# A filter's magnitude table shared between GpSimd and ScalarE, with a new order of the kernel's head

## The chip, the cores and the metric

The kernel runs on one core of a Trainium2 chip. A core has TensorE (matrix products, with its weight loads counted apart), VectorE, ScalarE and GpSimd for elementwise work, and SyncE, which here only issues DMAs; the profile calls them PE and PEld, DVE, ACT, POOL and SP. Each engine works through its own list of instructions in order and waits on semaphores for the others. The metric is device time in microseconds; the median of several runs is compared. Each kernel is also run once under the hardware profiler, and all rows shown come from such an execution.

## The reference

Two branches of a layer are added to the input. Both start from the same layer norm, over 2048 tokens of width 448.

```python
def _A_ref(u, log_A_real, A_imag, C_real, C_imag, log_dt, D_skip):
    dt = jnp.exp(log_dt)
    A = -jnp.exp(log_A_real) + 1j * A_imag          # [448, 256]
    C = (C_real + 1j * C_imag) * dt[:, None]
    P = jnp.exp((A * dt[:, None])[:, :, None] * pos[None, None, :])   # pos = 0 .. 2047
    K = 2.0 * jnp.einsum("dn,dnl->dl", C, P).real   # a filter of 2048 taps for each channel
    y = irfft(rfft(u_t, 2 * L) * rfft(K, 2 * L))[:, :, :L]
    return y + u * D_skip

def _B_ref(x, w_gate, w_up, w_down):                # width 448 -> 1792 -> 448
    h = _sigmoid(x @ w_gate) * (x @ w_up)
    return h @ w_down

xn = _layernorm(A_u)
return A_u + _A_ref(xn, ...) + _B_ref(xn, ...)
```

Everything is float32.

## The kernel before

Two Python generators, `conv()` (branch A) and `glu()` (branch B), are traced in turn, by weights that say how far each has come; a planner then works out the order of the instructions on every engine from the dependencies, the order of tracing, the priorities (`hp(HP)` raises them) and its own costs. `tc.issue_after(ins)` adds one rule by hand: what the block traces on the engine of `ins` is queued behind `ins`. So the order of each queue is fixed before the run, and it is worked out anew when an instruction changes.

**Head** (`conv`, from line 987). The tokens are handled in four groups of four blocks (a block is 128 tokens). `x_load` (232) brings a group into `accs[0]`, then `accs[1]`, one DMA for each 32 partitions; the first group's four go over SP and ScalarE's queue. On SP follow the gate and up weights of the first two slices of the hidden width (`w_load`), the down weights (`rd_load`), the parameters of the filter and groups 2 and 3. For groups 0 and 1 VectorE then takes mean and variance of each block (`x_stats`, 236), makes the scales with small steps that end in `zs` (`x_scales`, 253), and VectorE and ScalarE scale the blocks in turn (`x_norm`, 260 and 262). `x_transpose` (191) turns the group on TensorE; ScalarE copies the result to a rounded tile `xh` (or `xr`, 215, for the last 64 rows) and VectorE keeps the rest in `xl` (213, 216). A product is three matmuls with such pairs, high by high, high by low and low by high.

**Branch B** (`glu`, 691). For each of 14 slices f of the hidden width, `gate` (657) multiplies by the gate and up weights (670), ScalarE takes a tanh (678), VectorE forms `hf` and ScalarE and VectorE split it into `hh` and `hl` (686, 688). The down weights are split by ScalarE's `dh` (745) and GpSimd's `dl` (746) and multiplied later (777). In the first group of slices the order is f = 0, f = 1 for the first half of the tokens and then f = 0, f = 1 for the second, so that the second transposes are needed a little later. `marks[0]` is the latest tanh.

**Filter** (`prep`, then `kgen`, 434). `prep` turns the parameters into phases, gains `GG` and decays `W1` on VectorE, ScalarE and GpSimd. `kgen` then walks over 56 chunks of 8 channels. For each channel and state there is a decay r (one table of it in `me`, with the entries r^0 to r^63, and one in `mf`, with the gain times powers of r^64); `powers` (423) makes r^1, r^2, r^4 ... in `pm` for 8 chunks at a time, the row `pm[:, 6]` being filled with ones. `magnitudes` (469) makes the tables for two chunks on GpSimd: each step multiplies the finished half of the table by one power and so doubles it, with 1, 2, 4, 8, 16, 32 entries for each of 32 columns in `me` (w in the code). There are two buffers of `me` and `mf`. `ahead` (499) makes angles on TensorE (507) and sine and cosine in `S` on ScalarE (516 to 519). VectorE multiplies tables and S into `Et` (566, 567) and `Ft` (568), and TensorE contracts these over the states (578) into `ko`; every four chunks a first stage of the transform follows (534, 540). Chunks alternate with branch B's matmuls on TensorE's queue.

**Transform** (`spectra`, 799), from about 606 us: products of the spectra and the way back, together with the second half of branch B.

Of the kernel before, what the change touches and what calls it, by code (L numbers as in the profile page):

```python
# [47 lines left out]
DC = 8  # L48
# [82 lines left out]
def s4d_glu_kernel(ctx, tc, io):  # L131
# [59 lines left out]
    def x_transpose(src, xs, o0):  # L191
# [4 lines left out]
        for k in range(4):  # L196
# [10 lines left out]
            if k == 1 and nb == 2:  # L207
                p = ps.rearrange("p (k t) -> p k t", k=2)
                nc.scalar.copy(xh[:, 0:2, o], p)
                v.tensor_tensor(xl[:, 0:2, o], p, xh[:, 0:2, o], ALU.subtract)  # L210
            elif k < 3:
                nc.scalar.copy(xh[:, k, o], p)
                v.tensor_tensor(xl[:, k, o], p, xh[:, k, o], ALU.subtract)  # L213
            else:
                nc.scalar.copy(xr[0:64, o], p)
                xls[:] = [v.tensor_tensor(xr[64:128, o], p, xr[0:64, o], ALU.subtract)]

# [216 lines left out]
    def kgen(pk):  # L434
# [34 lines left out]
        def magnitudes(b):  # L469
# [16 lines left out]
            for m, base, nst in ((me, 0, 6), (mf, 7, 5)):  # L486
                for i in range(1 if m is mf else 0, nst):
                    w = 1 << i
                    with tc.issue_after(mls[0].ins) if mls else nullcontext():
                        ins = nc.gpsimd.tensor_tensor(  # L490
                            m[:, :, w : 2 * w],
                            m[:, :, 0:w],
                            par(base + i).unsqueeze(2).to_broadcast([128, 4 * DC, w]),
                            ALU.mult,
                        )
            mls[:] = [ins]
# [51 lines left out]
        nc.gpsimd.memset(mes[1][:, :, 0:1], 1.0)  # L548
        yield 4
        for g in range(NCK // NCH):  # L550
            for c in range(NCH):
# [3 lines left out]
                if c == 4 and NCH * (g + 1) < NCK:  # L555
                    if g == 0:
                        pms.append(pqs[0].tile([128, 12, NCH * 2 * DC], F32, name="pm1", tag="u0"))
                        nc.gpsimd.memset(pms[1][:, 6], 1.0)
                    with tc.issue_after(fts[0].ins):
                        powers(pms, g + 1)  # L560
# [12 lines left out]
                for q in range(2):  # L573
                    sl = 2 * (cn % 4) + q
                    for k in range(4):
                        h, cc = k // 2, k % 2
                        for j in range(4):
                            nc.tensor.matmul(  # L578
# [112 lines left out]
    def glu():  # L691
        for half in range(2):
# [4 lines left out]
            for fs_ in ORDER[half]:  # L697
# [14 lines left out]
                for n_, (f, t) in enumerate(order):  # L712
# [26 lines left out]
                    if t == 0:  # L739
                        dh = pg.tile([128, D], F32R, name="dh", bufs=FCH[0])  # L740
                        if half == 0:
                            rd = rd or rd_load(f)
                            dl = d_low()
                            with hp(HP), tc.issue_after(marks[0].ins):
# [232 lines left out]
    def conv():  # L977
        with tc.tile_pool(name="psk", bufs=1, space=PSUM) as ps_, tc.tile_pool(
# [9 lines left out]
            with tc.tile_pool(name="pst", bufs=1, side="right", reuse_waits="tile") as pst:  # L988
# [7 lines left out]
                x_load(accs[0], 0, 4, [nc.sync, nc.scalar])  # L996
# [10 lines left out]
                for q in range(2):  # L1007
                    xn = slots[f"xn{q}"]
                    with hp(HP):
                        for b in range(4 * q, 4 * q + 4):  # L1010
                            x_stats(sm, b, accs[q][:, b % 4])
# [55 lines left out]
    W1s, GGs = [], []  # L1067
# [43 lines left out]
```

## Time and profile before

| | |
|---|---|
| median of 3 runs | 799.61 us (797.79 to 801.61) |
| profiled execution | 803.19 us, span of its instructions 801.4 us |
| busy in the span | TensorE 716.8, VectorE 583.9, ScalarE 399.0, GpSimd 400.8 us |
| mean granted TensorE clock | 0.956 |
| head and preparation, 0 to 128 us | TensorE idle for about half of the first 40 us, then in one gap between 60 and 80 |
| chunk loop, 128 to 606 us | 28 table calls on GpSimd, 56 chunks |
| transform, 606 to 801 us | TensorE busy nearly throughout |

The busy time of an engine is the sum of its instructions; matmuls are pipelined, so a busy TensorE is not one at its peak. Rows by time give the start and length in us, the engine, the line of the kernel, the tiles (written <- read), the shape and in brackets the idle time before it with what ended it. In the chain of waits each moment is given to the instruction that the end of the work last waited for.

### The profile page before, as it was taken

Reading aid. Unit: us, or ns where it says so; the run is one execution under the profiler, and the core shown is the slowest. Engines: PE = TensorE matmul, PEld = TensorE weight load, DVE = VectorE, ACT = ScalarE, POOL = GpSimd, SP = SyncE. Lnnn points to the kernel's source line nnn. Section 1 sums busy time; section 2 is a strip of 40 time slices with the busy share of each in tenths; the row PEclk is TensorE's granted clock in tenths of the full one; section 3 lists DMA queues with packets and bytes.
Section 4 is the critical chain, followed back from the end, with each engine's and each line's share of the span. In section 5 each row is a group of like instructions: output and inputs, shape, how many; then the busy total and the mean of one; then the engine's idle time right before and its main releaser. Section 6 shows DMA issues by size and latency. Waiting matters only on the chain.

```text
span 801.4 us, 19239 instructions
## 1 busy us (share of the span) xinstructions
PE 716.8 (89%) x7892; PEld 563.5 (70%) x7892; DVE 583.9 (73%) x776; ACT 399.0 (50%) x594; POOL 400.8 (50%) x423
## 2 busy tenths in 40 slices
PE   1896998859798898969999899998999999998995
PEld 1674787648687787746587687787787777776783
DVE  4598996788897989888655977996794555545453
ACT  2645464654665765777626646754742332231320
POOL 1120055998855885884374568669364400243001
PEclk9997999959899999999899999999999999999998
DMA  9926347103522444434485132222145998999736
GB/s 208 226 76 180 103 133 225 38 15 127 165 85 67 150 147 119 118 93 147 119 239 174 62 97 90 64 85 91 59 133 167 285 246 218 227 233 258 179 110 167
DMA packets 90568, 114.74 MB, mean 143 GB/s; under 512 B 11825, under 2 KB 78577, under 8 KB 90225
## 3 DMA queue, kind: packets, MB, share of 16 engines
q1 hardware_dynamic: 81264, 92.78, 42.1%
q10 hardware_dynamic: 6640, 14.57, 6.0%
q0 software_dynamic: 2576, 6.17, 2.9%
q8 instruction: 62, 1.02, 0.5%
q14 instruction: 26, 0.20, 0.1%
HBM read 69.64 MB, written 43.84 MB: 142 GB/s over the span
## 4 chain that ended last, share of the span: by engine, by line
PE 52%; DVE 16%; POOL 9%; DMA 4%; issue 4%; ACT 4%; SPq 1%; ACTq 0%; POOLq 0%; DVEq 0%
PE gu L670 19%; PE po L777 13%; PE sp L859 6%; POOL me L490 5%; PE ko L578 5%; PE tr L507 4%; PE pv L886 3%; DVE Et L567 3%; DVE Ft L568 3%; POOL mf L490 2%; DVE pm L429 2%; DVE hl L688 1%; DVE Et L566 1%; PE gu L271 1%; DMA acc_d<-acc 1%
## 5 line engine op out<-in xcount | busy, mean ns | idle before, releaser
L490 POOL TENSOR_TENSOR me<-me,pm 128x32 f32<-128x32 f32 (+1 forms) x168 | 176.4, 1050 | 134.7 <-DVE Et L567 122.0
L490 POOL TENSOR_TENSOR mf<-mf,pm 128x64 f32<-128x64 f32 (+1 forms) x112 | 116.0, 1036 | 4.0
L566 DVE TENSOR_TENSOR Et<-me,S 128x1024 f32<-128x1024 f32 x56 | 84.9, 1516 | 44.2 <-ACT S L519 35.3
L670 PE MATMUL gu<-xh,wh 128*128 128x512 f32 x336 | 103.3, 414 | 3.9 <-DVE xl L213 3.2
L670 PE MATMUL gu<-xh,wl 128*128 128x512 f32 x336 | 99.2, 402 | 0.0
L670 PE MATMUL gu<-xl,wh 128*128 128x512 f32 x336 | 96.5, 393 | 0.0
L777 PE MATMUL po<-dh,hh 128*128 128x448 f32 x224 | 87.2, 389 | 1.8 <-DVE acc L782 1.8
L578 PEld LDWEIGHTS ko<-Et,Ft 128*32 128x32 f32 x3584 | 56.6, 115 | 43.8 <-issue 29.5
L516 ACT ACTIVATE S<-tr 128x1024 f32<-128x1024 f32 x56 | 57.3, 1024 | 59.5 <-PE tr L507 54.4
L578 PE MATMUL ko<-Et,Ft 128*32 128x64 f32 x3584 | 66.6, 228 | 22.3 <-DVE Ft L568 20.9
L568 DVE TENSOR_TENSOR Ft<-mf,S 128x1024 f32<-128x1024 f32 x56 | 83.8, 1496 | 2.0 <-POOL mf L490 2.0
L777 PE MATMUL po<-dl,hh 128*128 128x448 f32 x224 | 85.0, 379 | 0.0
L777 PE MATMUL po<-dh,hl 128*128 128x448 f32 x224 | 84.4, 378 | 0.0
L567 DVE TENSOR_TENSOR Et<-me,S 128x1024 f32<-128x1024 f32 x56 | 83.6, 1493 | 0.0
L688 DVE TENSOR_TENSOR hl<-hf,hh 128x512 fp32r<-128x512 f32 x56 | 58.9, 1052 | 26.6 <-ACT hh L686 26.6
L670 PEld LDWEIGHTS gu<-xh,wh 128*128 128x128 f32 x336 | 61.6, 192 | 23.5 <-issue 5.8
L507 PE MATMUL tr<-sel,ph 128*128 128x512 f32 x224 | 66.3, 419 | 11.3 <-ACT S L518 11.2
L670 PEld LDWEIGHTS gu<-xh,wl 128*128 128x128 f32 x336 | 65.2, 194 | 14.4
L686 ACT CAST hh<-hf 128x512 fp32r<-128x512 f32 x56 | 34.8, 622 | 80.2 <-DVE hf L681 71.1
L670 PEld LDWEIGHTS gu<-xl,wh 128*128 128x128 f32 x336 | 63.8, 190 | 13.7
L782 DVE SCALAR_TENSOR_TENSOR acc<-po,acc 128x448 f32<-128x448 f32 x80 | 48.1, 617 | 30.0 <-PE po L777 30.0
L678 ACT ACTIVATE th<-gu 128x512 f32<-128x512 f32 x56 | 33.5, 599 | 66.0 <-PE gu L670 58.8
(185 smaller groups left out, 1302.0 us busy)
## 6 DMA issues: line engine op xcount, KB each, us to landing
sk_d<-sk ACTq DMA_DIRECT2D x14, 512.0 KB
sx<-x_d SPq DMA_DIRECT2D x32, 224.0 KB
skl<-sk_d SPq DMA_DIRECT2D x16, 448.0 KB
vp<-v_d SPq DMA_DIRECT2D x16, 448.0 KB
v_d<-vt SPq DMA_DIRECT2D x62, 112.0 KB
wt_d<-wh SPq DMA_DIRECT2D x9, 512.0 KB
wt_d<-wl SPq DMA_DIRECT2D x9, 512.0 KB
wh<-wt_d SPq DMA_DIRECT2D x9, 512.0 KB
```

The source lines that it names most:

```text
L490: ins = nc.gpsimd.tensor_tensor(m[:, :, w : 2 * w], m[:, :, 0:w], par(base + i).unsqueeze(2).to_broadcast([128, 4 * DC, w]), ALU.mult,)
L507: nc.tensor.matmul(ps[:, h], ph[:, cn % 2, 128 * h : 128 * h + 128], sel[:, i], start=(i == 0), stop=(i == 1),)
L516: nc.scalar.activation(rows(cs), pv, AF.Abs)
L566: v.tensor_tensor(Et[:, :, :, 32:64], two(me[:, :, 32:64]), S[:, 1::-1], ALU.mult)
L567: v.tensor_tensor(Et[:, :, :, 0:32], two(me[:, :, 0:32]), S[:, 1:3, :, ::-1], ALU.mult)
L568: fts[:] = [v.tensor_tensor(Ft, two(mf), S[:, 3:5], ALU.mult)]
L578: nc.tensor.matmul(ko[32 * j : 32 * j + 32, sl], Ft[:, cc, DC * h + 4 * q + j], Et[:, cc, DC * h + 4 * q + j], start=(k == 0), stop=(k == ...
L670: glu_mm[:] = [nc.tensor.matmul(ps, a_, b_, start=(n == 0), stop=(n == len(mm) - 1))]
L688: v.tensor_tensor(hl, hf, hh, ALU.subtract)
L777: glu_mm[:] = [nc.tensor.matmul(po, a_[:, bs], w_, start=(n == 0), stop=(n == 3 * fc - 1))]
L782: v.scalar_tensor_tensor(acc[:, b], po, 0.5, acc[:, b], ALU.mult, ALU.add)
L859: mm = nc.tensor.matmul(to, tb[:kk, t, 64 * c : 64 * c + 64], rhs, start=True, stop=True, skip_group_check=True,)
```

## The change

Five edits.

- The first group's load becomes two loads of two blocks each, eight DMAs instead of four.
- The statistics of the second group are queued on VectorE behind the first group's norm (`normed` is the last of its scalings on VectorE).
- ScalarE's `dh` cast for f = 1 is queued behind ScalarE's last copy of the latest transpose (`act`) instead of behind the latest tanh.
- The second power table `pm1` is made, and its row of ones filled on GpSimd, ahead of the loop over chunks instead of in its fifth chunk.
- In `me`, the steps with w = 16 and w = 32 are done on GpSimd for the odd entries only (from the odd entries of the finished half, so both are read and written with a step of two elements). The even entries between w and 2w are the squares of the entries between w/2 and w, and ScalarE makes them with one Square each.

```diff
             else:
-                nc.scalar.copy(xr[0:64, o], p)
+                mv = nc.scalar.copy(xr[0:64, o], p)
                 xls[:] = [v.tensor_tensor(xr[64:128, o], p, xr[0:64, o], ALU.subtract)]
+                act[:] = [mv]
...
                 for i in range(1 if m is mf else 0, nst):
                     w = 1 << i
+
+                    a, n = (1, 2) if m is me and i > 3 else (0, 1)
                     with tc.issue_after(mls[0].ins) if mls else nullcontext():
                         ins = nc.gpsimd.tensor_tensor(
-                            m[:, :, w : 2 * w],
-                            m[:, :, 0:w],
-                            par(base + i).unsqueeze(2).to_broadcast([128, 4 * DC, w]),
+                            m[:, :, w + a : 2 * w : n],
+                            m[:, :, a:w:n],
+                            par(base + i).unsqueeze(2).to_broadcast([128, 4 * DC, w // n]),
                             ALU.mult,
                         )
+                    if n == 2:
+                        nc.scalar.activation(m[:, :, w : 2 * w : 2], m[:, :, w // 2 : w], AF.Square)
             mls[:] = [ins]
...
         nc.gpsimd.memset(mes[1][:, :, 0:1], 1.0)
+        pms.append(pqs[0].tile([128, 12, NCH * 2 * DC], F32, name="pm1", tag="u0"))
+        nc.gpsimd.memset(pms[1][:, 6], 1.0)
         yield 4
...
                 if c == 4 and NCH * (g + 1) < NCK:
-                    if g == 0:
-                        pms.append(pqs[0].tile([128, 12, NCH * 2 * DC], F32, name="pm1", tag="u0"))
-                        nc.gpsimd.memset(pms[1][:, 6], 1.0)
                     with tc.issue_after(fts[0].ins):
...
-                            nc.tensor.matmul(
+                            mm = nc.tensor.matmul(
                                 ko[32 * j : 32 * j + 32, sl],
...
-                            with hp(HP), tc.issue_after(marks[0].ins):
+                            with hp(HP), tc.issue_after((act if f == 1 else marks)[0].ins):
                                 nc.scalar.copy(dh, rd)
...
-                x_load(accs[0], 0, 4, [nc.sync, nc.scalar])
+                for b in (0, 2):
+                    x_load(accs[0][:, b : b + 2], b, 2, [nc.sync, nc.scalar])
...
                     with hp(HP):
-                        for b in range(4 * q, 4 * q + 4):
-                            x_stats(sm, b, accs[q][:, b % 4])
+                        with tc.issue_after(normed.ins) if q else nullcontext():
+                            for b in range(4 * q, 4 * q + 4):
+                                x_stats(sm, b, accs[q][:, b % 4])
                         x_scales(sm, 4 * q, 4)
...
-    W1s, GGs = [], []
+    W1s, GGs, act = [], [], []
```

## The prediction

> **What bounds the kernel now.** I read the busy line of the page first, then the busy time by stretches, then the chain of waits of the stretch that looked worst. In the rows by stretch the columns are the stretch, its length, then busy time of TensorE, its weight loads, VectorE, ScalarE and GpSimd, the granted clock, the DMA share and GB/s.
>
> ```profile
> PE 716.8 (89%) x7892; PEld 563.5 (70%) x7892; DVE 583.9 (73%) x776; ACT 399.0 (50%) x594; POOL 400.8 (50%) x423
> ...
> PE 52%; DVE 16%; POOL 9%; DMA 4%; issue 4%; ACT 4%; SPq 1%; ACTq 0%; POOLq 0%; DVEq 0%
> ...
> 60.00:80.00 20.00, 13.05 (x56) 8.30 (x54) 17.13 (x30) 10.96 (x16) 0.38 (x1) 0.74 0.66 179
> ...
> 148.00:168.00 20.00, 15.08 (x290) 11.21 (x288) 16.20 (x12) 12.87 (x17) 19.69 (x15) 0.83 0.14 44
> 168.00:188.00 20.00, 12.49 (x221) 10.04 (x222) 18.02 (x19) 11.23 (x15) 18.98 (x20) 0.74 0.09 32
> 188.00:208.00 20.00, 20.00 (x207) 16.17 (x207) 14.77 (x13) 12.25 (x18) 16.23 (x17) 1.00 0.57 187
> 200.00:300.00 100.00, 91.11 (x1217) 74.95 (x1219) 86.46 (x75) 63.10 (x86) 73.32 (x70) 0.93 0.38 124
> 300.00:400.00 100.00, 89.23 (x1321) 64.36 (x1320) 81.68 (x94) 68.35 (x104) 61.02 (x68) 0.93 0.40 117
> 400.00:500.00 100.00, 95.54 (x1267) 77.91 (x1256) 70.07 (x73) 55.37 (x77) 63.05 (x71) 0.98 0.44 135
> 500.00:606.00 106.00, 100.97 (x1449) 83.30 (x1447) 86.85 (x85) 60.33 (x80) 70.73 (x69) 0.98 0.27 84
> ```
>
> TensorE is busy for 716.8 of 801.4 us; a gain has to come out of the 84.6 us in which it is idle, or out of the low clock that follows an idle stretch (0.74 in 60 to 80 and in 168 to 188). The idle time is lumpy: 7.0 us in 60 to 80, 12.4 in 148 to 188, and 29.2 in the whole of 200 to 606 (8.9, 10.8, 4.5 and 5.0). So the head and the start of the chunk loop are where this change can earn, and the 400 us after them are where it can lose. The chain of waits in 128 to 215 shows who sets the pace at the start of the loop:
>
> ```profile
> by line: POOL me L490 39.3%; POOL mf L490 20.2%; issue 10.9%; DMA wraw<-in_B_w_up_dram 4.6%; POOL mf L480 3.6%; ACT wh L720 2.4%; DVE Ft L568 2.4%; POOL dl L746 2.2%; DVE Et L567 1.9%; DVE acc L782 1.8%; DVE hl L688 1.6%; DVE pm L429 1.5%;
> ```
>
> GpSimd's two magnitude tables (L490, L480) hold 63% of that stretch. Over the loop as a whole the waits (waiter, waited for, us in total, times, longest) look different:
>
> ```profile
> POOL me L490 <- DVE Et L567: 122.0, 21, 14.4
> ...
> DVE Et L566 <- ACT S L519: 35.3, 18, 6.4
> ...
> PE ko L578 <- DVE Ft L568: 20.9, 11, 3.8
> ```
>
> From 130 to 606, GpSimd waits 122.0 us for its table buffer to be read, VectorE waits 35.3 us, 18 times, for ScalarE's S, and TensorE waits 20.9 us for Ft. The change takes work from the engine that waits there and gives it to the one that is waited for.
>
> **The head, part by part.** These are rows in order of time (start, length, engine, line, and in brackets the idle time before and what ended it).
>
> ```profile
> 12.15 0.16 DVE L251 SCALAR_TENSOR_TENSOR ys<-z,ys 128x4 f32<-128x4 f32 x1
> 14.56 0.63 DVE L238 BATCH_NORM_STATS2 st<-acc 128x6 f32<-128x448 f32 x1 [2.24 <-DMA acc<-in_A_u_dram]
> 15.11 0.21 DVE L253 SCALAR_TENSOR_TENSOR zs<-mv,lim,ys 128x4 f32<-128x4 f32 x1
> ...
> 0.73 0.90 ACTq L234 DMA_DIRECT2D acc<-in_A_u_dram  x2
> ...
> 12.48 1.04 ACT L720 CAST wh<-wraw 128x1024 fp32r<-128x1024 f32 x1
> 15.35 1.41 ACT L262 ACTIVATE xn<-acc,zs,ys 128x448 f32<-128x448 f32 x2 [1.82 <-DVE zs L253]
> ...
> 35.60 0.56 ACT L745 CAST dh<-rd 128x448 fp32r<-128x448 f32 x1 [3.44 <-DMA rd<-in_B_w_down_dram]
> ...
> 17.43 3.65 PE L203 MATMUL gu<-ident,xn 128*128 128x128 f32 x16 [17.43 <-DVE xn L260]
> ...
> 37.42 2.49 PE L670 MATMUL gu<-xh,wh 128*128 128x512 f32 x6 [2.42 <-DVE xl L213]
> ...
> 40.14 1.44 PE L670 MATMUL gu<-xh,wl 128*128 128x512 f32 x3
> ...
> 42.55 0.84 PE L670 MATMUL gu<-xh,wl 128*128 128x512 f32 x3
> ```
>
> *Statistics of the second four blocks behind the first norm.* The scale of blocks 0 to 3 is ready at 12.31, but its last step (L253) stands behind a statistics instruction that waits until 14.56 for the second load, and starts at 15.11. Queued behind the norm, that wait goes: L253 at about 12.35, 2.8 us earlier. ScalarE's half of the norm (15.35) can then start when the weight cast ends at 13.52, or 1.8 us earlier at least; if it is put ahead of the cast, 2.8. I take 2.4 for the transposes that start at 17.43. What is late next is the second load itself: its statistics start on the same data at the same time as now and serve only the second group's transposes, so nothing is put on them.
>
> *First load in two halves.* Eight DMAs instead of four: two more issues on SP and two on ScalarE's queue, 0.90 us for two (the row at 0.73). SP's later loads, the first weights among them, slip by that much, and ScalarE has nothing to do so early. Bounds: 0.9 us late, to 1.3 early, because two of the four statistics (0.63 each) can run before the second half has landed. I take 0.
>
> *The down-projection cast of f = 1.* At 35.60 ScalarE casts dh after 3.44 us of waiting for its weights, and the last two xh copies stand behind it; TensorE's next gate matmul starts 2.42 us late at 37.42. The edit ties the cast behind the last copy of that transpose (L215), so this wait moves to where nothing is queued that TensorE needs at once. The idle 2.42 goes, and with it the slow clock behind it: six matmuls in 2.49 and three in 1.44, where three at full clock take 0.84, so 0.8 + 0.6 = 1.4. Together 3.8.
>
> The head is then 2.4 + 3.8 = 6.2 us earlier at 45 us. How much of this is left at 128, when the loop starts? The next lump stands between:
>
> ```profile
> 69.89 1.04 ACT L720 CAST wh<-wraw 128x1024 fp32r<-128x1024 f32 x1 [6.07 <-DMA wraw<-in_B_w_up_dram]
> ...
> 71.79 1.77 PE L271 MATMUL tr<-xn,wx 32*64 32x448 f32 x8 [6.94 <-ACT x1ab L282]
> ```
>
> That 6.94 us of idle time ends with a weight load from a queue of its own order, and VectorE is 17.1 of 20 us busy there with the filter's preparation. VectorE loses the same two waits, so it moves along, but the loads need not. Bounds 0 and 6.2; I take **-5**, nearer to the full amount because VectorE, not the load, sets the start of the loop.
>
> *Fill of ones for the second power table.* 0.20 us, moved ahead in the program:
>
> ```profile
> 92.03 0.20 POOL L558 MEMSET pm<- 128x128 f32 x1 [31.65 <-PE tr L271]
> ```
>
> It runs at 92 us today after 31.65 us of waiting for the buffer, in a stretch where GpSimd has next to no work. That idle time covers it; without the cover, in the loop, it costs its 0.2 us. Taken as 0. The unused name for a matmul does nothing.
>
> **The squares, part by part.** The table me is built in six steps, each doubling the one before. The two largest are halved on GpSimd (odd entries), and each gets a Square on ScalarE for the even ones. Grouped rows (count, busy us, mean ns):
>
> ```profile
> L490 POOL TENSOR_TENSOR me<-me,pm 128x1024 f32<-128x1024 f32 x28 | 62.7, 2239 | 0.3
> ...
> L490 POOL TENSOR_TENSOR me<-me,pm 128x512 f32<-128x512 f32 x28 | 36.4, 1301 | 0.6
> ...
> L490 POOL TENSOR_TENSOR me<-me,pm 128x256 f32<-128x256 f32 x28 | 23.0, 822 | 1.0
> ...
> L518 ACT ACTIVATE S<-tr 128x512 f32<-128x512 f32 x56 | 33.9, 605 | 0.0
> ...
> L212 ACT CAST xh<-gu 128x256 fp32r<-128x256 f32 x4 | 1.6, 406 | 0.1
> ...
> L348 ACT ACT_TABLE_LOAD x1 | 1.3, 1283 | 0.0
> ```
>
> GpSimd: 1024 becomes 512 (2239 to 1301 ns) and 512 becomes 256 (1301 to 822), 1.42 us less for each of 28 tables. ScalarE: Squares of 256 and 512 entries at about 406 and 605 ns, 1.0 us more for each.
>
> *At the start of the loop* GpSimd is 19.7 and 19.0 of 20 us busy, and the stall it causes is this:
>
> ```profile
> 172.96 0.40 ACT L427 ACTIVATE pm<-W,one 128x128 f32<-128x128 f32 x1 [7.96 <-POOL me L490]
> ...
> 175.72 1.65 PE L507 MATMUL tr<-sel,ph 128*128 128x512 f32 x3 [7.51 <-ACT S L518]
> ```
>
> ScalarE sits 7.96 us in front of an instruction that waits for the first step of the fourth table (last reader of the powers it overwrites), with S behind it, and TensorE sits 7.51 us behind S. Three tables are made before that: 3 x 1.42 = **-4.3**. The two tables after it save 2.8 more, but TensorE is busy for all of 188 to 208, so this is hidden. Bounds: -7.1 (all five count) and 0, where the new Squares wait in ScalarE's queue for GpSimd and S waits behind them as it does now.
>
> *After 200* some 23 tables remain. A Square waits for GpSimd's step, and behind it in ScalarE's queue stand S, th and hh. Of 56 first products Et, 18 wait for S (0.32), and of the 35.3 us that VectorE waits there TensorE sees 20.9 (0.59). So 23 x 1.0 x 0.32 x 0.59 = +4.3. Against it stands what GpSimd's shorter work gives back to VectorE:
>
> ```profile
> L566 DVE TENSOR_TENSOR Et<-me,S 128x1024 f32<-128x1024 f32 x56 | 84.9, 1516 | 44.2 <-ACT S L519 35.3
> ...
> L566 DVE TENSOR_TENSOR Et<-me,S x56: 1207/1262/3033, 141.8 to 597.4; 128x1024 f32<-128x1024 f32 x56
> ```
>
> The mean is 1516 ns, the median 1262, so the 46 x 3 products after 200 lose 138 x 0.254 = 35 us, I take it to collisions with GpSimd. GpSimd is busy there for 268 us (the four rows above) and 33 of them go, 12%: 4.3 us less on VectorE. VectorE has 16% of the chain at 73% busy, so 0.22 of this counts, -0.9. Sum after 200: **+3.4**; bounds -4.3 and +13.6 (every Square in front of an awaited S: 23 x 1.0 x 0.59).
>
> *Reading every second entry.* No row has this step of 8 bytes; the nearest one reads two rows 128 elements apart (L480), beside a dense step of the same 64 elements (L490, least of min/median/max):
>
> ```profile
> L490 POOL TENSOR_TENSOR mf<-mf,pm x112: 303/1062/2120, 141.2 to 584.0; 128x64 f32<-128x64 f32 x28, 128x128 f32<-128x128 f32 x28, 128x256 f32<-128x256 f32 x28, 128x512 f32<-128x512 f32 x28
> ...
> L480 POOL TENSOR_TENSOR mf<-GG,pm x28: 312/317/1310, 139.0 to 576.1; 128x64 f32<-128x64 f32 x28
> ```
>
> 317 against 303 ns: a stride costs next to nothing, so I keep the halves as priced. [...]
>
> **Sum.** -5 - 4.3 + 3.4 = -5.9 us. The profiled execution took 803.19 us in all (span 801.4), so 797.3 for it; the median of the runs, 799.61, stands 3.6 lower, and -5.9 from there is **793.7**.
>
> **The rivals.**
> 1. *Slower: ScalarE's queue becomes the bound.* Place: the Square in front of the next chunk's S. Every Square delays an awaited S (+13.6), GpSimd's start-of-loop saving is lost to the same waits (0), the relief stays (-0.9), the head stays (-5): +7.7, 807.3. For it speaks that ScalarE's S is what VectorE waits for most, and that ScalarE already sits 7.96 us behind GpSimd once. Against it, that ScalarE is idle for about a third of each stretch after 200. It decides once each table after 200 holds TensorE back by more than 9.3 + 0.9 = 10.2 us / 23 = 0.44 us.
> 2. *The head's gain is given back* by 128, at the load of 69.89: 0 - 4.3 + 3.4, 798.7.
> 3. *Squares run in idle time* and all five early tables count: -6.2 - 7.1 - 0.9 = -14.2, 785.4.
> 4. *The change doesn't do what it says:* Square needs another function table than Sin and Tanh. Two loads of 1.28 us for each of 28 calls are 72 us, above 860. The trace has three such loads, one at each of three lines (one is shown); that Abs, Sin, Tanh and plain copies are mixed freely after them speaks against it.
> [...]
>
> **How the numbers follow.** Forecast 0.34, rivals 0.28, 0.17, 0.14, 0.02 and 0.05. 0.5% is 4.0 us, about what a measurement of this kernel can tell from no change: faster is below 795.6, slower above 803.6. Faster: 0.26 of the forecast, 0.14 of the third, 0.06 of the second and fifth: 0.46. Slower: 0.25 of the first, 0.02 of the fourth, 0.03 of the forecast and the second: 0.30. The rest, 0.24, is the same. The range runs from the third case with early bounds and the whole relief (-6.2 - 7.1 - 4.3 = -17.6, 782) to the first with some reordering on top (810). The forecast's own range is 788 to 799.
>
> **What would show it.** Right: transposes start near 15 us instead of 17.4; no gap ahead of the gate matmuls near 35; the loop's first table step on GpSimd about 5 us earlier; GpSimd's largest me rows at 512 entries and 0.8 to 1.3 us; the 7.5 us gap of TensorE near 170 down to about 3. Wrong: ScalarE's wait for GpSimd above 15.0 us in the loop, VectorE's wait for S above 35.3, TensorE's wait for Ft above 20.9, or TensorE idle for more than 29 us after the loop's start-up. What would upset all of it is another order of the queues: the instruction order is worked out anew from the changed costs.

## The result, and the profile after

The changed kernel took 798.60 us (median of 20 runs, 790.13 to 802.61) against 801.54 us for the kernel before (20 runs, 797.79 to 806.91) on the same chip. The ratio is 0.9935 with a 95% interval of 0.9912 to 0.9958: about 5 us faster. The profiled execution has a span of 798.3 us against 801.4. Executions of one kernel differ by several us here, so a difference of 3 us between two traces alone proves little, and the trace of each stage is read beside the ratios of the runs.

The page of the changed kernel, its busy line and the chain that ended last:

```profile
PE 720.1 (90%) x7892; PEld 562.2 (70%) x7892; DVE 549.7 (69%) x776; ACT 424.4 (53%) x650; POOL 334.0 (42%) x423
...
PE 51%; DVE 19%; POOL 8%; ACT 6%; DMA 6%; issue 5%; SPq 3%; DVEq 0%; POOLq 0%; ACTq 0%
```

GpSimd is 66.8 us less busy and ScalarE 25.4 more. The steps that the edit halves account for 45.2 of the 66.8 us (122.1 before, 76.9 after; the rows stand in the prediction and below), and 17 us came off the steps of `mf`, which the edit doesn't touch. VectorE, which the edit doesn't touch in the loop, is 34.2 us less busy. TensorE is idle for 78.2 us instead of 84.6, but its busy time has grown by 3.3. The stretches of the changed kernel, with the columns of the prediction's first fence:

```profile
60.00:80.00 20.00, 14.49 (x75) 9.44 (x68) 18.28 (x36) 13.48 (x19) 0.00 (x0) 0.91 0.50 133
148.00:168.00 20.00, 11.10 (x214) 7.89 (x213) 14.44 (x13) 12.62 (x18) 14.91 (x17) 0.78 0.13 43
168.00:188.00 20.00, 16.83 (x239) 13.65 (x240) 18.00 (x20) 14.13 (x20) 17.75 (x19) 0.83 0.21 80
...
200.00:300.00 100.00, 91.32 (x1343) 74.14 (x1342) 79.12 (x85) 70.04 (x101) 61.26 (x76) 0.98 0.37 123
300.00:400.00 100.00, 92.83 (x1197) 64.27 (x1198) 69.68 (x84) 70.01 (x111) 49.41 (x66) 0.88 0.39 119
400.00:500.00 100.00, 94.45 (x1238) 77.91 (x1237) 63.20 (x70) 59.35 (x86) 48.17 (x68) 0.97 0.40 124
500.00:606.00 106.00, 99.29 (x1472) 81.31 (x1474) 80.07 (x85) 65.19 (x91) 54.05 (x67) 0.98 0.27 87
```

GpSimd no longer fills 148 to 188 (14.9 and 17.8 of 20 us instead of 19.7 and 19.0), yet TensorE is idle for 12.1 us there, about as long as before (12.4). In 300 to 400 the granted clock is 0.88 instead of 0.93. The waits of the changed kernel from 125 to 606 us (waiter, waited for, us in total, times, longest):

```profile
POOL me L493 <- DVE Et L571: 174.6, 24, 15.2
...
DVE Et L570 <- ACT S L524: 69.8, 27, 6.7
...
ACT me L500 <- POOL me L493: 44.3, 29, 5.4
...
ACT pm L428 <- POOL me L493: 6.7, 3, 5.2
...
PE ko L582 <- DVE Ft L572: 12.4, 11, 2.5
```

There is a new wait of 44.3 us: ScalarE's Squares (L500) wait 29 times for GpSimd's halves. VectorE's wait for ScalarE's S has doubled, 35.3 to 69.8. TensorE's wait for Ft has fallen all the same, 20.9 to 12.4. One place at the start of the loop shows how the first two are tied, in rows by time, ScalarE first:

```profile
155.44 0.43 ACT L500 ACTIVATE me<-me 128x256 f32<-128x256 f32 x1 [3.08 <-POOL me L493]
155.77 0.57 ACT L682 ACTIVATE th<-gu 128x512 f32<-128x512 f32 x1
157.27 0.64 ACT L500 ACTIVATE me<-me 128x512 f32<-128x512 f32 x1 [0.93 <-POOL me L493]
157.81 1.00 ACT L521 ACTIVATE S<-tr 128x1024 f32<-128x1024 f32 x1
```

and TensorE, which makes the next angles only when S has read the last ones:

```profile
160.27 2.08 PE L512 MATMUL tr<-sel,ph 128*128 128x512 f32 x4 [6.86 <-ACT S L523]
```

Two Squares that wait for GpSimd stand in ScalarE's queue ahead of S, and TensorE sits idle for 6.86 us behind S.

**Where the time went, by stage.** The copy `ks` closes every fourth chunk; there are 14. The table cuts the profiled execution of each kernel at the start of the 1st, 6th and 14th `ks`. Up to each cut the kernels do the same work: from the 6th to the 14th, TensorE has 3450 to 3454 matmuls in each kernel whose rows for that stage are shown below. Lengths in us; the experiments are explained in the next section.

| kernel | to 1st ks | 1st to 6th | 6th to 14th | after 14th | span | ratio of the runs to before |
|---|---|---|---|---|---|---|
| before | 176.6 | 162.2 | 267.4 | 195.2 | 801.4 | 1 |
| changed | 172.0 | 161.1 | 271.7 | 193.5 | 798.3 | 0.9935 (0.9912 to 0.9958) |
| e1 head only | 169.0 | 162.3 | 274.0 | 195.0 | 800.3 | 1.0022 (0.9994 to 1.0050) |
| e2 Squares only | 173.2 | 164.8 | 267.5 | 194.8 | 800.3 | 1.0002 (0.9969 to 1.0035) |
| e3 head, odd halves, no Squares | 167.4 | 152.7 | 270.8 | 195.6 | 786.5 | 0.9749 (0.9704 to 0.9795) |
| e4 changed, Squares behind S | 166.6 | 150.0 | 270.8 | 193.3 | 780.7 | 0.9804 (0.9762 to 0.9846) |
| e5 head only, first load whole | 172.0 | 162.3 | 265.2 | 193.8 | 793.3 | 0.9936 (0.9905 to 0.9968) |
| e6 load in halves only | 170.6 | 162.1 | 277.2 | 192.9 | 802.8 | 1.0013 (0.9986 to 1.0039) |
| e7 as e4, first load whole | 168.4 | 151.3 | 268.3 | 195.0 | 783.0 | 0.9771 (0.9728 to 0.9814) |
| e8 as e4, old head | 170.4 | 154.4 | 273.0 | 195.0 | 792.8 | 0.9941 (0.9911 to 0.9970) |
| e9 as e4, Squares in 32 chunks | 166.3 | 150.0 | 266.1 | 198.7 | 781.1 | 0.9730 (0.9685 to 0.9775) |
| e10 as e9, first load whole | 168.0 | 150.7 | 268.2 | 193.2 | 780.2 | 0.9761 (0.9712 to 0.9809) |
| e11 changed, first load whole | 173.7 | 159.7 | 271.5 | 194.2 | 799.1 | 0.9943 (0.9902 to 0.9983) |

The changed kernel leads by 4.6 us at the first `ks` and by 5.7 at the sixth, and has given back 4.3 of that at the fourteenth.

How far one execution can be trusted: e1 and e6 have the same instructions in the same order on every engine (see e6), and their stages still differ by 1.6, 0.2, 3.2 and 2.1 us. Nor is the profiled execution always a typical one: that of e3 (788.32 us) lies 7.4 us above the median of e3's runs (780.93), and that of e4 (782.47) 5.0 below its own (787.47).

### The profile page after: what moved, and what is told of

It reads as the page before. It is cut to its first block, busy times and chain, and to the rows that moved or that the text cites. A ratio compares the mean times of both kernels' runs of the same rounds, so it can differ in the third digit from the quotient of the medians.

```text
span 798.3 us, 19353 instructions
## 1 busy us (share of the span) xinstructions
PE 720.1 (90%) x7892; PEld 562.2 (70%) x7892; DVE 549.7 (69%) x776; ACT 424.4 (53%) x650; POOL 334.0 (42%) x423
## 4 chain that ended last, share of the span: by engine, by line
PE 51%; DVE 19%; POOL 8%; ACT 6%; DMA 6%; issue 5%; SPq 3%; DVEq 0%; POOLq 0%; ACTq 0%
PE gu L674 21%; PE po L781 9%; PE sp L863 6%; PE ko L582 4%; POOL me L493 4%; DVE Et L571 4%; PE tr L512 4%; PE pv L890 3%; DVE Ft L572 3%; DVE pm L430 2%; DVE wl L728 1%; PE gu L272 1%; DVE acc L786 1%; DVE Et L570 1%; DVE hf L685 1%
## 5 line engine op out<-in xcount | busy, mean ns | idle before, releaser
L493 POOL TENSOR_TENSOR me<-me,pm 128x32 f32<-128x32 f32 (+1 forms) x168 | 132.5, 789 | 186.6 <-DVE Et L571 174.6
L570 DVE TENSOR_TENSOR Et<-me,S 128x1024 f32<-128x1024 f32 x56 | 73.7, 1315 | 76.7 <-ACT S L524 69.8
L493 POOL TENSOR_TENSOR mf<-mf,pm 128x64 f32<-128x64 f32 (+1 forms) x112 | 99.0, 884 | 4.2
L674 PE MATMUL gu<-xh,wl 128*128 128x512 f32 x336 | 97.0, 398 | 0.0
L781 PE MATMUL po<-dh,hh 128*128 128x448 f32 x224 | 86.7, 387 | 3.5 <-DVE hf L685 1.6
L781 PE MATMUL po<-dl,hh 128*128 128x448 f32 x224 | 83.6, 373 | 0.7 <-POOL dl L750 0.7
L781 PE MATMUL po<-dh,hl 128*128 128x448 f32 x224 | 83.2, 374 | 0.0
L571 DVE TENSOR_TENSOR Et<-me,S 128x1024 f32<-128x1024 f32 x56 | 80.5, 1438 | 0.0
L582 PE MATMUL ko<-Et,Ft 128*32 128x64 f32 x3584 | 66.3, 226 | 12.5 <-DVE Ft L572 12.4
L692 DVE TENSOR_TENSOR hl<-hf,hh 128x512 fp32r<-128x512 f32 x56 | 54.3, 969 | 33.6 <-ACT hh L690 33.6
L572 DVE TENSOR_TENSOR Ft<-mf,S 128x1024 f32<-128x1024 f32 x56 | 75.1, 1342 | 0.7 <-PE ko L582 0.7
L524 ACT ACTIVATE S<-S,hpi 128x1024 f32<-128x1024 f32 x56 | 65.2, 1164 | 0.8 <-ACT hh L690 0.8
```

The costliest lines, as they stand in the source:

```text
L493: ins = nc.gpsimd.tensor_tensor(m[:, :, w + a : 2 * w : n], m[:, :, a:w:n], par(base + i).unsqueeze(2).to_broadcast([128, 4 * DC, w // n]) ...
L524: nc.scalar.activation(cs, cs, AF.Sin, scale=-TWO_PI, bias=hpi)
L570: v.tensor_tensor(Et[:, :, :, 32:64], two(me[:, :, 32:64]), S[:, 1::-1], ALU.mult)
L571: v.tensor_tensor(Et[:, :, :, 0:32], two(me[:, :, 0:32]), S[:, 1:3, :, ::-1], ALU.mult)
L572: fts[:] = [v.tensor_tensor(Ft, two(mf), S[:, 3:5], ALU.mult)]
L582: mm = nc.tensor.matmul(ko[32 * j : 32 * j + 32, sl], Ft[:, cc, DC * h + 4 * q + j], Et[:, cc, DC * h + 4 * q + j], start=(k == 0), stop=( ...
```

## The experiments

**e1, the new head without the Squares.** The table is built on GpSimd alone, as before; the rest of the change stays.

```diff
-                    a, n = (1, 2) if m is me and i > 3 else (0, 1)
+                    a, n = 0, 1
```

(with n at 1 the Squares behind `if n == 2` are never traced)

> The changed kernel with all six steps of the table me whole on GpSimd again and no Square: the head's edits and the moved fill alone. Theory A (the head earns, the squares cost a little): 5 to 8 us less than before, a ratio of 0.990 to 0.994, and the chunk loop starts about 6 us earlier. Theory B (the head's gain is given back, the squares earn): a ratio of 0.998 to 1.002. Theory C (the gain is a lucky order of the queues that only the five edits together give): any ratio above 0.996.

Measured: ratio 1.0022, just above theory B's range and within C's. The head earns nothing that can be measured, although it leads by 7.6 us at the first `ks`. The lead is whole at the sixth (331.3 against 338.8 us) and 0.9 us at the fourteenth.

**e2, the Squares without the new head.** The kernel before, with the change's loop over the steps (the diff of the section on the change, from `a, n =` to `AF.Square`) and nothing else.

> The kernel before with only the odd entries on GpSimd and the even ones as Squares on ScalarE. Theory A: between 1 us less and 5 us more, a ratio of 0.999 to 1.006, with ScalarE waiting for GpSimd some 40 us in the loop. Theory B: 4 to 6 us less, 0.993 to 0.996. Theory C: the ratios of this run and of the head alone don't multiply to that of the whole change (0.9935).

Measured: ratio 1.0002, as theories A and C had it; the Squares wait 57.6 us for GpSimd in the loop. The Squares alone earn nothing either: they lead by 3.4 us at the first `ks` (173.2 against 176.6) and by 0.8 at the sixth. The product of the two ratios, 1.0024, is not the 0.9935 of the whole change, so the two parts don't simply add.

**e3, what GpSimd's relief is worth.** The changed kernel with GpSimd's odd halves and no Squares; the even entries of the two larger steps stay at one, so the table is another one.

```diff
-        nc.gpsimd.memset(mes[0][:, :, 0:1], 1.0)
+        nc.gpsimd.memset(mes[0], 1.0)
...
-                    if n == 2:
-                        nc.scalar.activation(m[:, :, w : 2 * w : 2], m[:, :, w // 2 : w], AF.Square)
...
-        nc.gpsimd.memset(mes[1][:, :, 0:1], 1.0)
+        nc.gpsimd.memset(mes[1], 1.0)
```

> The changed kernel without the Squares: GpSimd makes the odd entries of the two larger steps, the even ones stay at one, so the table is not the right one and 28 x 2 instructions of ScalarE are gone; both table buffers are filled with ones at the start. This is GpSimd's relief without its price on ScalarE. Theory A: clearly below the head alone, 3 to 8 us, a ratio of 0.982 to 0.990. A rival, that GpSimd is not the bound even at the start of the loop: within 2 us of the head alone.

Measured: ratio 0.9749, below theory A's range. On TensorE, ScalarE, VectorE and SyncE the instructions stand in e1's order, so e1 and e3 differ by GpSimd's shorter steps, by the two longer fills at the start (1.8 us each) and by the values in the table. GpSimd is 38.9 us less busy (394.4 to 355.5), VectorE 23.0 (584.0 to 561.0), and the kernel is 2.7% faster (0.9749 over 1.0022). The relief of GpSimd is by far the largest term in this study. From the 1st to the 6th `ks`, in e1 and then in e3:

```profile
169.00:331.30 162.30, 150.20 (x2105) 123.38 (x2105) 141.30 (x131) 102.48 (x141) 120.53 (x119) 0.93 0.37 120
```

```profile
167.40:320.10 152.70, 145.14 (x2105) 119.27 (x2105) 130.04 (x131) 102.97 (x140) 108.38 (x119) 0.97 0.39 128
```

TensorE is idle for 7.6 us instead of 12.1, at a granted clock of 0.97 instead of 0.93: 9.6 us in 20 chunks. The values in the table are not what does it there: e4, below, has the right table, the same clock of 0.97 and an even shorter stage. Nor is it that the tables come sooner, as the rows of the first product Et show, for the whole span in e1 and then in e3:

```profile
L570 DVE TENSOR_TENSOR Et<-me,S 128x1024 f32<-128x1024 f32 x56 | 82.7, 1478 | 41.0 <-ACT S L524 30.4 <-POOL me L493 7.4 <-POOL mf L493 2.9
```

```profile
L568 DVE TENSOR_TENSOR Et<-me,S 128x1024 f32<-128x1024 f32 x56 | 80.0, 1429 | 44.6 <-ACT S L522 31.2 <-POOL mf L493 10.0 <-POOL me L493 3.2
```

VectorE waits no less for GpSimd's tables (13.2 us instead of 10.3); it is its own instructions that got shorter.

**e4, the Squares behind the sines.** The changed kernel, with each Square queued behind the last sine that has been traced so far, which is that of the next chunk.

```diff
-            nc.scalar.activation(cs, cs, AF.Sin, scale=-TWO_PI, bias=hpi)
+            sls.append(nc.scalar.activation(cs, cs, AF.Sin, scale=-TWO_PI, bias=hpi))
...
                     if n == 2:
-                        nc.scalar.activation(m[:, :, w : 2 * w : 2], m[:, :, w // 2 : w], AF.Square)
+                        with tc.issue_after(sls[-1].ins) if len(sls) >= 1 else nullcontext():
+                            nc.scalar.activation(m[:, :, w : 2 * w : 2], m[:, :, w // 2 : w], AF.Square)
```

> The changed kernel with each Square queued on ScalarE behind the sine and cosine S of the next chunk, so that no Square waits for GpSimd with that S behind it. If the Squares' waits in ScalarE's queue are what costs: 2 to 5 us less than the changed kernel, a ratio of 0.987 to 0.991. If it is ScalarE's added busy time: within 2 us of the changed kernel (0.991 to 0.996). If the table now comes too late for the products: slower than the changed kernel, with VectorE's wait for the table above 10 us.

Measured: ratio 0.9804, below the range of its first case, median 787.47 us. The same stage in the changed kernel (with the next stage, for later) and then in e4:

```profile
172.00:333.10 161.10, 147.24 (x2108) 119.21 (x2107) 129.85 (x136) 111.78 (x161) 101.37 (x116) 0.97 0.37 122
333.10:604.80 271.70, 257.99 (x3450) 200.36 (x3450) 183.65 (x206) 170.88 (x254) 128.77 (x176) 0.94 0.35 108
```

```profile
166.60:316.60 150.00, 146.33 (x2108) 119.53 (x2107) 128.91 (x135) 111.22 (x161) 109.93 (x120) 0.97 0.40 131
```

The engines do the same work; TensorE's idle time falls from 13.9 to 3.7 us. So from the 1st to the 6th `ks` the Squares at their own place cost what GpSimd's relief brings (161.1 against e3's 152.7, +8.4), and behind the sines they cost nothing there. It is so in every kernel with the new head: 150.0 to 151.3 us in the four with the Squares behind the sines (e4, e7, e9, e10), 161.1 and 159.7 in the two with the Squares at their own place (changed, e11). Up to the first `ks` it is the same: 172.0 against e3's 167.4, and 166.6 in e4. The planner's order of the queues differs between the changed kernel and e4 in other places too, so the whole of 0.9804 over 0.9935 isn't shown to come from this one wait. Over the whole kernel e4 is not the equal of e3: 0.9804 against 0.9749, with intervals that overlap. From the 8th to the 14th `ks` e4 takes 192.7 us and e3 181.3.

**e5 and e6, why the head alone earned nothing.** Behind the first chunks, e1's order on TensorE is that of the kernel before in all of the loop but one stretch: from 371 to 465 us of e1, just behind the 7th `ks` to just behind the 9th (the expectations of e5 and e6 say chunk, where they should say `ks`; of the lead of 7.5 us, the rows that e5's names show 5.4 lost there, not 6.6). The time goes between the 7th and the 8th `ks`: 54.8 us in e1, 45.8 in the kernel before. e5 is e1 with the load whole; e6 is the kernel before with the load in halves and nothing else. In the traces e5 has the old order on TensorE from 130 us on, and e6 has e1's order on every engine from the first instruction to the last (by operation, tiles and shapes). So the load in halves alone brings the other order, and the other three edits of the head change nothing more in any queue once it is there.

```diff
-                for b in (0, 2):
-                    x_load(accs[0][:, b : b + 2], b, 2, [nc.sync, nc.scalar])
+                x_load(accs[0], 0, 4, [nc.sync, nc.scalar])
```

(for e5; e6 has the same lines the other way round, put into the kernel before)

> The new head without the Squares, as in the run of the head alone, but the first load stays whole. With the load in halves the order in which the program was built differs from that of the kernel before not only in the head but once more, on TensorE between the 7th and the 9th chunk of the loop, and there the run of the head alone lost 6.6 of the 7.5 us that it led by (the copies ks at 331.3 against 338.8 us, at 419.8 against 421.9). With the load whole TensorE's order after the head is that of the kernel before. Theory A (the other order costs the lead): the lead at the first ks stays to the end; 5 to 7 us faster than before, ratio 0.991 to 0.994. Theory B (the lead is lost there in any order, because TensorE is full from 370 to 420 us): ratio 0.999 to 1.003.

> The kernel before with one part of the change alone, the first load in two halves. It brings the other order between the 7th and the 9th chunk, without the statistics' place and the early cast that bring the head's lead. Theory A: the head gains 0 to 1.5 us by the halves and the loop loses about 6.6, so 5 to 6.5 us slower than before, ratio 1.006 to 1.008. Theory B: the ratio is 0.999 to 1.001.

Measured: e5 0.9936, theory A; e6 1.0013, between the two. From the 6th to the 14th `ks`, in the kernel before, e1, e5 and e6:

```profile
338.80:606.20 267.40, 250.14 (x3454) 195.96 (x3453) 203.69 (x210) 158.64 (x226) 168.24 (x178) 0.97 0.36 110
```

```profile
331.30:605.30 274.00, 253.28 (x3454) 196.27 (x3453) 204.30 (x210) 158.40 (x225) 164.71 (x178) 0.96 0.35 108
```

```profile
334.30:599.50 265.20, 248.51 (x3454) 193.11 (x3453) 204.00 (x210) 158.88 (x226) 168.75 (x178) 0.97 0.36 111
```

```profile
332.70:609.90 277.20, 255.03 (x3454) 197.74 (x3453) 204.61 (x210) 158.33 (x225) 164.83 (x178) 0.95 0.34 106
```

The same 3454 matmuls take 267.4 and 265.2 us in the old order, 274.0 and 277.2 in the other: 9.3 us on the mean, for a part of the program that no edit touches. Between the 7th and the 8th `ks` alone it is 45.8 and 46.5 us against 54.8 and 55.5 (and 56.1 in e3, which has e1's order). About half of the 9.3 us is idle time of TensorE (20.7 us in e1, 16.7 in e5) and about half a longer busy time at a lower granted clock. From the 1st to the 6th `ks`, where the order is the same in all four, they take 162.2, 162.3, 162.3 and 162.1 us. e6's own expectation missed because the halves gain more in the head than either theory had allowed: 6.0 us at the first `ks` (170.6 against 176.6), which pays for most of what the other order takes.

**e7 and e8, the parts crossed.** e7 is e4 with the first load whole (the diff of e5). e8 is the Squares behind the sines with the old head (e2 with the diff of e4).

> The changed kernel with each Square queued behind the last sine of the next chunk and the first load whole. Theory A in its strong form (the loss between the 7th and the 9th chunk comes with the load in halves whatever else is changed): up to 6.6 us better than the run with the Squares behind the sines and the load in halves, ratio 0.972 to 0.976. If the Squares reorder that stretch anyway (its stage from the 7th to the 8th ks took 45.8 us, not 54.8): the same as that run, ratio 0.978 to 0.984.

> The kernel before with its own head, and the Squares, each queued behind the last sine of the next chunk. If the head's lead of 7.5 us is worth its whole amount once the Squares hold nothing up: 7 us slower than the run with the new head and the Squares behind the sines, ratio 0.988 to 0.990. If the head earns nothing, as it did alone: ratio 0.978 to 0.983.

Measured: e7 0.9771, between its two cases, its interval overlapping e4's (0.9804); e8 0.9941, slower even than its first case. With the Squares out of the way the new head is worth 1.4% (0.9804 over 0.9941), more than its lead of 3.8 us at the first `ks`: e8 also takes 4.4 us longer to the sixth and 2.2 to the fourteenth. What those 6.6 us are isn't settled; the order of the queues differs there too.

**e9 and e10, the Squares in the first 32 chunks only.** From the 8th `ks` on, GpSimd builds the table alone again.

```diff
-                    a, n = (1, 2) if m is me and i > 3 else (0, 1)
+                    a, n = (1, 2) if m is me and i > 3 and b < 16 else (0, 1)
```

> The run with the Squares behind the sines, with the Squares in the tables of the first 32 of the 56 chunks only; the later tables are built by GpSimd alone as before. Between the 8th and the 14th ks that run took 192.7 us (394.7 to 587.4), the kernel before 184.3 (421.9 to 606.2) and the new head alone 185.5. Theory A (the Squares' time in ScalarE's queue is what lengthens the second half): 7 to 8 us better than that run, ratio 0.970 to 0.972. Theory B (the second half is longer because of the order in which the program was built, or because TensorE arrives there earlier and then waits for something else): the same as that run, ratio 0.978 to 0.984.

> The same with the first load whole: the run with the load whole and the Squares behind the sines, with the Squares in the first 32 chunks only. There the stretch from the 8th to the 14th ks took 187.4 us, 3.1 more than in the kernel before. Theory A: 2 to 3 us better than that run, ratio 0.973 to 0.975. Theory B: the same, 0.975 to 0.980.

Measured: e9 0.9730, near its first case, with a median of 780.41 us; e10 0.9761. The interval of e9 touches those of e4 and e7, so that it beats both kernels is shown, and that it beats e4 only likely. From the 6th to the 14th `ks` e9 took 266.1 us against e4's 270.8, for theory A, but e10 took 268.2 against e7's 268.3, for theory B, and e1 and e6 show that one order can differ by 3.2 us in that stage. Whether the Squares themselves lengthen the second half of the loop stays open.

**e11, the changed kernel with the first load whole.** The diff of e5 on the changed kernel.

> The changed kernel as it is, Squares at their own place in ScalarE's queue, with the first load whole. If the halves bring the bad order in the changed kernel too, it gains what the head alone gained by the whole load (0.9936 against 1.0022): ratio 0.984 to 0.987. If the Squares have already put TensorE's queue into another order (its stage from the 7th to the 8th ks took 45.8 us, not 54.8), it only loses what the halves brought to the head, 172.0 against 169.0 us at the first ks: ratio 0.994 to 0.998.

Measured: ratio 0.9943, its second case. In the changed kernel the Squares have put TensorE's queue into a third order, and there the halves neither cost nor bring anything that can be measured. So the order that cost e1 its lead is not in the changed kernel.

## Why the prediction was right in its total, and wrong in its parts

The forecast was 5.9 us faster; the runs show 0.65%, about 5.2 us, and the two profiled spans 3.1. (The 793.7 us stood on 799.61, the median of 3 runs; 20 runs put the kernel before at 801.54 and the changed one at 798.60.) That the total came out near is luck. At the first `ks` the sum had the changed kernel 9.3 us ahead and the traces have 4.6; after 200 it had 3.4 lost, with two terms that were wrong by a factor, in opposite directions.

*The head, -5 at 128 us.* The size was about right, the way to it was not. Rows by time of the changed kernel, VectorE, ScalarE and TensorE:

```profile
11.79 0.22 DVE L254 SCALAR_TENSOR_TENSOR zs<-mv,lim,ys 128x4 f32<-128x4 f32 x1
...
14.67 1.68 DVE L239 BATCH_NORM_STATS2 st<-acc 128x6 f32<-128x448 f32 x3 [0.49 <-issue]
```

```profile
12.11 1.41 ACT L263 ACTIVATE xn<-acc,zs,ys 128x448 f32<-128x448 f32 x2
...
30.86 0.59 ACT L215 CAST xr<-gu 64x512 fp32r<-64x512 f32 x1
35.90 0.57 ACT L749 CAST dh<-rd 128x448 fp32r<-128x448 f32 x1 [4.46 <-DMA rd<-in_B_w_down_dram]
```

```profile
12.62 3.68 PE L203 MATMUL gu<-ident,xn 128*128 128x128 f32 x16 [12.62 <-DVE xn L261]
...
29.07 0.63 PE L203 MATMUL gu<-ident,xn 128*64 128x128 f32 x4 [1.49 <-ACT th L682]
30.78 1.65 PE L674 MATMUL gu<-xh,wh 128*128 128x512 f32 x3 [1.09 <-DVE xl L213]
...
70.81 1.36 PE L272 MATMUL tr<-xn,wx 32*64 32x448 f32 x8 [1.96 <-ACT x1ab L283]
...
171.17 2.08 PE L512 MATMUL tr<-sel,ph 128*128 128x512 f32 x4 [3.76 <-ACT S L523]
```

The scales are ready at 11.79 instead of 15.11 and the transposes start at 12.62, 4.8 us earlier; the forecast was 2.4 (bounds 1.8 to 2.8). The term that was mis-sized is the load in halves, taken as 0 with bounds of +0.9 to -1.3: alone (e6) it takes the wait for the second group's load out of the scales' way and puts the cast behind the last copy, so that it has e1's order, and the edits that the sum priced at 2.4 and 3.8 add nothing to it. The leads of e6 and e1 at the first `ks`, 6.0 and 7.6 us, are two executions of one order; without the halves the other edits bring 4.6 (e5). The cast of f = 1 now waits 4.46 us behind the last copy, where it holds nothing up, and the gap of 2.42 us near 35 is gone, as forecast, but gaps of 0.48, 1.49 and 1.09 us stand between 26 and 31 us in its place. After the same 98 matmuls of the head TensorE is 4.4 us ahead (39.76 against 44.14 us), where the sum had 6.2: the early transposes are all of it, and the 3.8 us of the cast did not come. The next lump, TensorE's 6.94 us at 71.8, didn't take the gain back but shrank to 1.96 us (at 70.81), and the loop's first table step starts 4.4 us earlier (125.1 against 129.5).

*Squares at the start of the loop, -4.3 (bounds -7.1 to 0).* This step failed as a term to be added to the head's. On the new head the Squares made it 3.0 us worse to the first `ks` (172.0 against e1's 169.0; 1.7 with the load whole, e11 against e5), outside the bounds; on the old head they brought 3.4 (e2), near the forecast. GpSimd's halves alone are worth -1.6 on the new head (e3), no more than two executions of one order differ by, and the Squares' waits in front of S cost +4.6 (172.0 against 167.4), as the rows at 155.44 and 160.27 show. The lower bound of 0 had named this very wait, "the new Squares wait in ScalarE's queue for GpSimd and S waits behind them", but had priced it as if it could only cancel the gain. The old stall of 7.51 us did shrink as forecast, to 3.76 (at 171.17), and another of 6.86 came ahead of it.

*After 200, +4.3 for the Squares and -0.9 for GpSimd's relief.* Both are far too small. In the 20 chunks between the 1st and the 6th `ks` alone the relief is worth 9.6 us (e3 against e1) and the Squares cost 8.4 (changed against e3). Of the relief, the first factor failed: 12% of the 35 us that it took for collisions with GpSimd were to come off VectorE, 4.3 us, and 33.0 came off from 200 to 606 us (325.1 to 292.1). The 35 us were those of the three products alone; from e1 to e3 these lost 11.7 us of their 251.4, and other work of VectorE (`hl`, `pm`) 10.8 more. The second, the 0.22 by which the relief was scaled down, failed as well: from the 1st to the 6th `ks` e3 had 11.3 us off VectorE (141.3 to 130.0) and took 9.6 less. Grouped rows of the changed kernel:

```profile
L570 DVE TENSOR_TENSOR Et<-me,S 128x1024 f32<-128x1024 f32 x56 | 73.7, 1315 | 76.7 <-ACT S L524 69.8 <-POOL me L493 4.2 <-POOL mf L493 2.5
...
L493 POOL TENSOR_TENSOR me<-me,pm 128x256 f32<-128x256 f32 x56 | 42.9, 767 | 1.6
...
L493 POOL TENSOR_TENSOR mf<-mf,pm 128x512 f32<-128x512 f32 x28 | 40.6, 1450 | 2.1
L493 POOL TENSOR_TENSOR me<-me,pm 128x512 f32<-128x512 f32 x28 | 34.0, 1213 | 0.4
...
L500 ACT ACTIVATE me<-me 128x512 f32<-128x512 f32 x28 | 18.9, 674 | 9.5 <-POOL me L493 9.4
L500 ACT ACTIVATE me<-me 128x256 f32<-128x256 f32 x28 | 12.3, 438 | 39.1 <-POOL me L493 34.9 <-DVE acc L786 4.3
```

The first product Et takes 1315 ns instead of 1516. From the 6th to the 14th `ks` the changed kernel is 4.3 us slower than the one before, with less idle time of TensorE (13.7 us against 17.3) and more busy time (258.0 against 250.1) at a granted clock of 0.94 against 0.97. So in this execution what the forecast had as waiting after 200 came, from the 6th `ks` on, as a lower clock.

*The prices of one table* were good: GpSimd's steps from 4.36 us (2239, 1301 and 822 ns) to 2.75 (1213 and twice 767), 1.6 less against 1.42; ScalarE 1.1 more (438 and 674 ns) against 1.0.

*The rivals.* The first, the Square in front of the next S, has its mechanism: 8.4 us over the ten tables of that stage are 0.84 us a table, above its threshold of 0.44, and ScalarE's wait for GpSimd (51.0 us in two rows) and VectorE's wait for S (69.8) crossed the marks set for it. The other two marks were kept: TensorE waits 12.4 us for Ft, and is idle for 28.1 us from 200 to 606. The time did not follow, since the relief that it left at -0.9 was ten times that. The third, Squares in idle time, is what e4 makes of them: 787.5 against the 785.4 written down. The second, the head's gain given back, didn't happen at 71.8 us but did in e1, 300 us later and by the order of a queue. The fourth didn't happen: the trace has three loads of function tables as before (1.28 us each). As for the fifth, which has a chance of 0.05 in the forecast, no run shows that a step over every second entry is dearer on GpSimd: with 512 entries it takes 1271 ns in e3 where the dense one takes 1264 in e1, and at least 1052 ns in the changed kernel where the dense one takes at least 1048 in the kernel before. (The row of L480, on which the forecast leant, was too short to tell, and its 317 ns is a median set beside a least of 303: in the kernel before a step of 32 entries takes 271 ns at least, so 32 more cost some 30.)

*The last sentence of the prediction*, that another order of the queues would upset all of it, had no chance of its own in the numbers; it decided e1, by about 9 us (265.2 against 274.0 in e5 and e1).

## What to carry to other kernels

Before work is moved from one engine to another, measure the two halves by themselves: the relief of the first engine with the moved work left out (e3), and the moved work at a place where nobody waits behind it (e4); here the relief was worth 2.7%, the moved work then cost about 0.6% (0.9804 over 0.9749, with intervals that overlap), and the change as written netted 0.65%. An instruction that waits for another engine belongs in its queue behind what others wait for, not ahead of it: here the stage from the 1st to the 6th `ks` took 150.0 us with the Squares behind S (e4) and 161.1 with them ahead of it (changed). Where a planner orders the queues, follow a lead by milestones through the whole kernel and compare the orders of the two programs, since an edit in the head can cost 9 us in a stretch that it doesn't touch; and compare them before two edits are credited apart, since they may give one and the same order.

## What the runs showed of the hardware

**A long half clock in a stretch where TensorE is busy.** Stretches of the changed kernel in the stage around the 7th `ks`:

```profile
365.00:370.00 5.00, 4.41 (x24) 2.55 (x22) 5.00 (x8) 2.48 (x6) 1.31 (x1) 1.00 0.92 306
370.00:375.00 5.00, 4.35 (x72) 1.91 (x70) 3.46 (x7) 5.00 (x9) 0.00 (x0) 0.67 0.22 53
375.00:380.00 5.00, 5.00 (x17) 2.55 (x12) 2.87 (x4) 2.79 (x6) 3.45 (x7) 0.50 0.25 54
380.00:385.00 5.00, 5.00 (x64) 3.92 (x65) 2.43 (x3) 2.44 (x5) 3.20 (x5) 0.50 0.43 95
385.00:390.00 5.00, 5.00 (x88) 3.79 (x85) 1.34 (x3) 2.52 (x5) 0.00 (x0) 0.63 0.26 105
```

TensorE's gaps there are 0.45, 0.37 and 0.28 us long, in the rows that have an idle time:

```profile
368.25 2.08 PE L272 MATMUL gu<-xt,wx 32*64 32x448 f32 x8 [0.45 <-DVE hf L685]
370.70 0.77 PE L582 MATMUL ko<-Et,Ft 128*32 128x64 f32 x40 [0.37 <-DVE Ft L572]
371.74 0.64 PE L203 MATMUL gu<-ident,xt 128*64 128x128 f32 x2 [0.28 <-DVE xl L213]
```

After them the granted clock stays at about a half for some 16 us, although TensorE is busy for all of 375 to 390. At these clocks the four rows from 370 lose an estimated 8.3 us of matmul time (4.35 x 0.33, twice 5 x 0.5, 5 x 0.37), more than the whole change earned. The estimate takes a matmul's time to go as one over the clock; the `po` matmuls (L781) start 0.20 us apart at 366.6 to 367.4, at 1.00, and 0.37 apart at 379.4 to 380.9, at 0.50. Why the clock stays low for so long isn't settled here. The gaps need not be the cause: the eight matmuls of the first row took 2.08 us at a granted clock of 1.00, where eight of the same form took 0.98 at 359.51, so TensorE did less there than its busy time says. Nor is it this kernel alone: e3 has 0.50 from 360 to 380 us, e5 and e6 from 375 to 385, with TensorE busy throughout. e4 has the clock at 0.98 from its 6th to its 8th `ks`, with no such stretch. That many of these matmuls are of small tiles (32*64 and 128*32 in the rows above) is a rival that no run tests.

**VectorE is slowed by GpSimd even where neither waits for the other.** With the order of VectorE's queue unchanged (e1 to e3), 38.9 us less work on GpSimd took 23.0 us off VectorE, 0.6 us for each. The single instructions show it too: of the 168 products Et and Ft in e1's trace, the 57 with next to no GpSimd instruction beside them (under 5% of their length) take 1216 ns on the mean, the 55 with GpSimd busy beside them for 95% or more take 1860. In the trace of the kernel before the same two groups are 54 at 1218 ns and 58 at 1846. What it is in the hardware that slows them, no trace shows.
